# A fused attention and FFN kernel: the order of the FFN's products fixed from step 28 on instead of step 96, and a block's output evicted in two halves

## The chip, the cores and the metric

The kernel runs on one core of one Trainium2 chip. The metric is the device time of one execution in microseconds. Before the change the median of three runs is 952.14 us (951.54 to 952.98).

## The reference

The kernel computes a local and a downsampled attention over `q`, `k`, `v` (8 batches, 8 heads, 576 positions, 64 features per head), adds the two, and runs the result through a feed-forward network with a squared ReLU. All data is float32.

```
def _attn_ref(q, k, v):
    factor = 4
    q_d, k_d, v_d = ...                      # means over groups of 4 positions
    out_d = sm_attn(q_d, k_d, v_d)           # full softmax attention over 144 positions
    out_up = np.repeat(out_d, factor, axis=2)
    mask = np.abs(pos[:, None] - pos[None, :]) < factor
    scores = scale * np.matmul(q, k.transpose(0, 1, 3, 2))
    scores = np.where(mask, scores, -1000000000.0)
    ...                                      # softmax
    return out_up + np.matmul(attn, v)

def _moe_ref(x, w_in, w_out, s, b):          # x: 4608 x 512, w_in: 512 x 2048
    h = x @ w_in
    r = np.maximum(h, 0.0)
    g = s * (r * r) + b
    return g @ w_out
```

## The kernel before

**Tiling of the FFN.** The 4608 rows are cut into 18 blocks `t` of 256 rows, the 2048 hidden features into 8 parts `p` of 256. A *step* is one pair (t, p); `order` lists the 144 steps, from step 24 on simply block after block, 8 steps each, beginning with block 3. To keep float32 precision each operand is split into a high and a low float32r part, and a product is computed as three matmuls (high x high, high x low, low x high).

**One step** consists of four pieces of work, each a Python generator that a "stream" hands out in small units:

- `G`, the first products (`products1`, line 631): 24 matmuls of 256 columns into one PSUM bank `ph`. From block 3 on (with one exception in step 25) even steps use bank 4 and odd steps bank 6.
- `R` (`upper`, lines 646 to 648): ReLU, square and a rounding copy to `gh` on ScalarE. Every third step writes its pair (`gh`, `gl`) to a tile named `gb`.
- `V` (`lower`, line 653): the remainder `gl` on VectorE; after it the `ph` bank is free.
- `H`, the second products (`products2`, lines 707 to 709): 12 matmuls of 512 columns, six for the first 128 rows of the block (m = 0, PSUM bank 0 from block 3 on) and six for the other 128 rows (m = 1, bank 1). They add up over the 8 steps of a block. `H` of a step is issued one or more steps after its `G`, since `R` and `V` lie in between.

After the last `H` of a block, `evict` (line 685) computes the two halves of the output tile `os` out of the two banks with one VectorE operation each, and one DMA on SP's queue (line 687) writes the 512 KB block. The next block's products use the same two banks. The last block has an eviction of its own (line 716), in quarters.

**Attention** runs beside this. For batches 0 to 2 it is done by small matmuls (`banded`). For batches 3 to 7 the local part is done on GpSimd and VectorE (`local_unit`: GpSimd multiplies at line 537, VectorE sums at line 539, and so on), transposed by TensorE at line 569 (`ot`), and the downsampled part uses TensorE at line 342 (`sa`), lines 365 to 370 (`tp`, `tr`) and lines 381 to 383 (`up`). Before a block enters the FFN, `split_x` (lines 612 and 613) makes the high and low part of its input.

**What sets the order.** Three regimes follow one another:

1. A written plan, the string `PLAN`. Each word advances one stream; `d`, `v` and `l` with a number are pieces of attention of that unit, `G`, `R`, `V`, `H` the FFN's. `in_order` chains all instructions of TensorE, VectorE, ScalarE and GpSimd as written. The plan holds 56 `G` and 56 `H`, all of steps 0 to 27, with two units of each per step. Block 2's eviction lies in it, at the second `H` of step 23.
2. From `planned` = 28 up to `BEGIN` = 96 the loop with `until` emits the work step by step, `H` two steps behind, and the framework's planner, which simulates a timeline, decides the order on each engine by priority and simulated readiness. The first ten steps carry a dependency that puts them behind the plan (`behind_plan`).
3. From `BEGIN` on the loop runs over pairs of steps, and `products` chains TensorE's FFN matmuls in the order of emission. From here a step's `G` comes in three units (3, 9 and 12 matmuls) and its `H` in four units of 3. A pair is: 3 of `G`, 3 of `H`, 21 of `G`, 3 of `H`, 24 of `G` (the second step's), 18 of `H`. The planner still places attention's matmuls between these.

In all regimes `advance` emits attention at a rate set by the step number, and the order on each engine is fixed when the program is built.

Of the kernel before, what the change touches and what calls it, by code (L numbers as in the profile page):

```python
# [11 lines left out]
F32 = mybir.dt.float32  # L12
# [4 lines left out]
ALU = mybir.AluOpType  # L17
AX = mybir.AxisListType

P = 128  # L20
B, H, S, D = 8, 8, 576, 64
# [3 lines left out]
DM = H * D  # L25
# [11 lines left out]
TB = 256  # L37
NB = NT // TB
NFP = DFF // 256
# [47 lines left out]
def attention_ffn_kernel(ctx, tc, qk, vw_in, vr_in, vdm, qkn, vn, w_in, w_out, s_in, b_in, out):  # L87
    nc = tc.nc
# [3 lines left out]
    def pool(name, bufs, gap=0):  # L92
        if gap:
            ctx.enter_context(tc.tile_pool(name="gap_" + name, bufs=1)).tile(
                [P, gap // 4], F32, name="gap")
        return ctx.enter_context(tc.tile_pool(name=name, bufs=bufs))
# [4 lines left out]
    xp = pool("xp", 2, 0)  # L101
    xp1 = pool("xp1", 1)
# [7 lines left out]
    def bank(i, shape, name):  # L110
        return ps.tile(shape, F32, tag=f"k{i}", name=name)
# [98 lines left out]
    bias = cst.tile([P, DM], F32, name="bias")  # L210
# [408 lines left out]
    oacc = {}  # L619
# [3 lines left out]
    def products1(t, p):  # L623
# [3 lines left out]
        for j in range(2):  # L627
            f = slice(P * j, P * j + P)
            for k in range(NK):
                for s, xk in ((0, xh), (0, xl), (1, xh)):  # L630
                    nc.tensor.matmul(  # L631
                        ph[:, j], wi[p][:, s, k, f], xk[:, k],
                        start=k == 0 and s == 0 and xk is xh, stop=k == NK - 1 and s == 1)
                if j == 0 and k == 0 and order.index((t, p)) >= BEGIN:
                    yield
# [36 lines left out]
    def column_sums():  # L672
# [3 lines left out]
        nc.vector.tensor_scalar(bias, cs, sb_b, None, ALU.mult)  # L676
        yield

    def evict(t):
        if t < 2:  # L680
            os_ = xp.tile([P, 2, DM], F32, tag="xh", name="os")
        else:
            os_ = xp1.tile([P, 2, DM], F32, tag="os", name="os")
        for i in range(2):
            nc.vector.scalar_tensor_tensor(  # L685
                os_[:, i], oacc[t][i], sb_s, bias, ALU.mult, ALU.add)
        nc.sync.dma_start(
            out[TB * t : TB * t + TB, :].rearrange("(m p) c -> p m c", p=P), os_)

    def gemm2(t, p):  # L690
        for _ in products2(t, p):
            pass

    def products2(t, p):
        gh, gl = gt.pop((t, p))
        if p == 0:
            ob = OB.get(t, OB[0])
            oacc[t] = [bank(i, [P, DM], "po") for i in ob]
        po = oacc[t]
        end = t == NB - 1 and p == NFP - 1  # L700
        os_ = xp1.tile([P, 2, DM], F32, tag="os", name="os") if end else None
        for m in range(2):
            ms = slice(P * m, P * m + P)
            for j in range(2):
                first = p == 0 and j == 0
                last = p == NFP - 1 and j == 1
                nc.tensor.matmul(po[m], gh[:, j, ms], wo[p][:, 0, j], start=first, stop=False)  # L707
                nc.tensor.matmul(po[m], gh[:, j, ms], wo[p][:, 1, j], start=False, stop=False)  # L708
                nc.tensor.matmul(po[m], gl[:, j, ms], wo[p][:, 0, j], start=False, stop=last)  # L709
                if j == 0 and order.index((t, p)) >= BEGIN - 2:  # L710
                    yield
            if end:
                r0 = TB * t + P * m
                for c in (0, DM // 2):
                    cs = slice(c, c + DM // 2)
                    nc.vector.scalar_tensor_tensor(
                        os_[:, m, cs], po[m][:, cs], sb_s, bias[:, cs], ALU.mult, ALU.add)
                    nc.sync.dma_start(out[r0 : r0 + P, cs], os_[:, m, cs])
            elif p == NFP - 1 and m == 1 and t >= 2:
                evict(t)  # L720
            yield


# [11 lines left out]
    tail = {}  # L735
# [19 lines left out]
    def begin_x():  # L755
        for t in range(2):
            xs[t] = tuple(
                xp.tile([P, HP, TB], F32R, tag=tag, name=tag) for tag in ("xh", "xl"))
        for hs in (slice(0, HP - 1), slice(HP - 1, HP)):
            for t in range(2):  # L760
                xh, xl = xs[t]
                src = xt[0][:, hs, t * TB : t * TB + TB]
                nc.scalar.copy(xh[:, hs], src)
                yield
                nc.vector.tensor_tensor(xl[:, hs], src, xh[:, hs].bitcast(F32), ALU.subtract)  # L765
                yield

    def third_x():
        xs[2] = xh, xl = tuple(
            home[tag].tile([P, HP, TB], F32R, tag=tag, name=tag) for tag in ("os", "xl2"))  # L770
        for b, src, dst in ((0, slice(2 * TB, S), slice(0, S - 2 * TB)),
                            (1, slice(0, 3 * TB - S), slice(S - 2 * TB, TB))):
            nc.scalar.copy(xh[:, :, dst], xt[b][:, :, src])
            yield
            nc.vector.tensor_tensor(
                xl[:, :, dst], xt[b][:, :, src], xh[:, :, dst].bitcast(F32), ALU.subtract)
            yield

    def fourth_x():
        xs[3] = xh, xl = tuple(  # L780
            xp.tile([P, HP, TB], F32R, tag=tag, name=tag) for tag in ("xh", "xl"))
        src = xt[1][:, :, 3 * TB - S : 4 * TB - S]
        nc.scalar.copy(xh, src)
        yield
        nc.vector.tensor_tensor(xl, src, xh.bitcast(F32), ALU.subtract)
        yield

    BEGIN = 96
    order = [(t, p) for p in range(HF) for t in range(2)]
    order += [(2, 0), (2, 1)] + [(t, HF) for t in range(2)]  # L790
    order += [(2, p) for p in range(2, NFP)]
# [6 lines left out]
    sb_s = cst.tile([P, 1], F32, name="sb_s")  # L798
# [23 lines left out]
    streams = {"x": begin_x(), "y": third_x(), "z": fourth_x(), "b": add_rows()}  # L822
# [21 lines left out]
    plan = PLAN.split()  # L844
# [10 lines left out]
    @contextlib.contextmanager  # L855
    def behind_plan():

        traced = nc.cur_bb.bb.instructions
        last = traced[-1]
        yield  # L860
        start = next(k for k in reversed(range(len(traced))) if traced[k] is last) + 1
        for i in traced[start:]:
            if i.engine in ENGINES:
                tc.add_manual_dep(
                    i, tail[i.engine].name,
                    mybir.DependencyInfo(
                        mybir.DependencyClass.NoSync, mybir.DependencyReason.DATA),
                    reason="behind_plan")

    gone = {kind: plan.count(kind) for kind in "GRVH"}  # L870

    def until(kind, count):
        while gone[kind] < count:
            next(streams[kind])
            gone[kind] += 1

    chain_end = None

    def products(kind, count):

        nonlocal chain_end
        for _ in range(count):
            traced = nc.cur_bb.bb.instructions
            last = traced[-1]
            next(streams[kind])
            start = next(k for k in reversed(range(len(traced))) if traced[k] is last) + 1
            for i in traced[start:]:
                if i.engine == nc.tensor.engine:
                    if chain_end:
                        tc.add_manual_dep(  # L890
                            i, chain_end.name,
                            mybir.DependencyInfo(
                                mybir.DependencyClass.NoSync, mybir.DependencyReason.DATA),
                            reason="products")
                    chain_end = i

    def finish(st):
        with tc.high_priority():
            next(streams["R"])
            next(streams["V"])  # L900
        advance(st + 0.5)
# [32 lines left out]
    def advance(st):  # L934
        nonlocal done
        while done < target(st):
            with tc.high_priority(offset=300 if done < NY[1] else 60 if done < NY[1] + NY[2] else 0):
                if next(gen, "end") == "end":
                    break
            done += 1  # L940
# [3 lines left out]
    def split(st):  # L944
        if order[st] in splits:
            split_x(splits[order[st]])

    planned = gone["G"] // 2
    for st in range(planned, BEGIN):
        with behind_plan() if st < planned + 10 else contextlib.nullcontext():  # L950
            until("G", 2 * st + 2)
            with tc.high_priority():
                until("R", st + 1)
                until("V", st + 1)
            advance(st + 0.5)
            until("H", 2 * (st - 2))
            advance(st + 1)
            split(st)
    until("H", 2 * BEGIN - 4)
    for st in range(BEGIN, len(order), 2):  # L960
        products("G", 1)
        products("H", 1)
        products("G", 2)
        finish(st)
        products("H", 1)
        advance(st + 1)
        split(st)
        products("G", 3)
        finish(st + 1)
        products("H", 6)  # L970
        advance(st + 2)
        split(st + 1)
    products("H", 8)


# [60 lines left out]
```

## Time and profile before

| | |
|---|---|
| median of 3 runs | 952.14 us |
| profiled execution, its own time | 951.88 us |
| its span, first to last instruction | 949.8 us |
| TensorE busy | 926.5 us |
| VectorE busy | 641.0 us |
| ScalarE busy | 479.1 us |
| GpSimd busy | 410.7 us |
| mean granted TensorE clock | 0.998 |

In the profile PE is TensorE's matmuls, PEld its weight loads, DVE is VectorE, ACT ScalarE, POOL GpSimd and SP SyncE, which issues the DMAs. Times in rows are microseconds from the start of the span. A row of the chain of waits is start, length, and what the time went to; a row of instructions in order of time is start, busy time, engine, line, operation, and in brackets the idle time of the engine before it with what ended it. A row that groups instructions by line ends in count, busy microseconds, mean nanoseconds of one, and idle time before them. A row of a stage is its start and end, its length, each engine's busy time with the count of instructions, and at the end the granted clock, the share of the DMA engines that is busy, and GB/s. `ph<-xh,wi` means that `ph` is written from `xh` and `wi`. Ends of matmuls are modelled and overlap the next, so intervals between starts tell the rate.

### The profile page before, as it was taken

To read this page: it belongs to the slowest core of one execution; us is meant where nothing else is said; L and a number is where in the kernel's file an instruction comes from. 1 tells how busy PE (TensorE), PEld (TensorE's weight loads), DVE (VectorE), ACT (ScalarE), POOL (GpSimd) and SP (SyncE) were. 2 spreads that over 40 slices of the span, in tenths; PEclk is the share of its full clock that TensorE was granted. 3 is DMA by queue.
4 is the path that set the end of the run, shared out by engine and by line. 5 is a ranking of instruction groups with operands and counts; after the bars stand their busy time and mean duration, and the time that the engine had idled before them with its cause. 6 is when DMAs were issued, how large, how long until landed. Compare 5 with 4: busy or idle time off the path is not lost.

```text
span 949.8 us, 18419 instructions
## 1 busy us (share of the span) xinstructions
PE 926.5 (98%) x7316; PEld 836.1 (88%) x7316; DVE 641.0 (67%) x1134; ACT 479.1 (50%) x1133; POOL 410.7 (43%) x440
## 2 busy tenths in 40 slices
PE   6699999999999999999999999999999999999998
PEld 5588888788899999999999999999999999999996
DVE  9999999855587878787878888877887521111111
ACT  7977774466563635445454545453535333233331
POOL 6401130010577676766676877667777200000000
PEclk9999999999999999999999999999999999999999
DMA  9755413122232322323232323241312000000000
GB/s 325 268 163 191 145 46 119 50 89 91 96 118 89 118 90 86 121 80 107 80 115 92 120 87 118 67 133 51 127 62 70 1 23 1 23 1 23 1 23 22
DMA packets 31751, 86.25 MB, mean 91 GB/s; under 512 B 3249, under 2 KB 7857, under 8 KB 31665
## 3 DMA queue, kind: packets, MB, share of 16 engines
q1 hardware_dynamic: 31664, 85.08, 27.2%
q8 instruction: 57, 0.93, 0.4%
q14 instruction: 30, 0.24, 0.1%
HBM read 75.63 MB, written 9.44 MB: 90 GB/s over the span
## 4 chain that ended last, share of the span: by engine, by line
PE 85%; DVE 8%; POOL 3%; ACT 2%; issue 1%; DMA 1%; DVEq 0%; POOLq 0%; ACTq 0%
PE ph L631 38%; PE po L707 13%; PE po L708 13%; PE po L709 13%; PE sa L342 2%; PE up L383 1%; POOL pr L537 1%; PE ot L569 1%; PE ol L479 1%; DVE es L272 1%; PE up L381 1%; PE sl L436 1%; DVE es L273 1%; PE tr L370 1%; DVE gl L653 1%
## 5 line engine op out<-in xcount | busy, mean ns | idle before, releaser
L631 PE MATMUL ph<-xh,wi 128*128 128x256 f32 x2176 | 413.5, 281 | 0.1
L631 PEld LDWEIGHTS ph<-xh,wi 128*128 128x128 f32 x2176 | 344.2, 189 | 6.8 <-DVE gl L653 0.5
L631 PE MATMUL ph<-xl,wi 128*128 128x256 f32 x1152 | 322.7, 280 | 0.0
L537 POOL TENSOR_TENSOR pr<-lqk 128x576 f32<-128x576 f32 x140 | 199.0, 1444 | 76.3 <-DMA lqk<-in_qkn_dram 52.5
L631 PEld LDWEIGHTS ph<-xl,wi 128*128 128x128 f32 x1152 | 218.4, 190 | 5.9 <-DVE xl L765 0.3
L646 ACT ACTIVATE ph<-ph 128x512 f32<-128x512 f32 x144 | 83.8, 582 | 241.3 <-PE ph L631 240.8
L707 PE MATMUL po<-wo,gh 128*128 128x512 f32 x416 | 166.0, 399 | 0.7 <-DVE os L685 0.3
L708 PE MATMUL po<-wo,gh 128*128 128x512 f32 x416 | 163.8, 394 | 0.0
L709 PE MATMUL po<-wo,gl 128*128 128x512 f32 x416 | 162.6, 392 | 1.0 <-DVE gl L653 0.9
L559 POOL TENSOR_TENSOR acc<-acc,pv 128x576 f32<-128x576 f32 x80 | 117.3, 1466 | 56.7 <-DVE acc L559 30.2
L653 DVE TENSOR_TENSOR gl<-ph,gh 128x512 fp32r<-128x512 f32 x104 | 71.2, 685 | 103.9 <-ACT gh L648 103.4
L539 DVE TENSOR_REDUCE st<-pr 128x9 f32<-128x576 f32 x140 | 106.0, 757 | 38.8 <-POOL pr L537 36.3
L558 DVE TENSOR_TENSOR pv<-lv,st 128x576 f32<-128x576 f32 x120 | 86.9, 747 | 17.4 <-POOL acc L559 16.9
L312 POOL TENSOR_TENSOR dq<-vt 80x64 f32<-80x64 f32 x58 | 22.6, 401 | 174.6 <-PE up L383 173.1
L709 PEld LDWEIGHTS po<-wo,gl 128*128 128x128 f32 x416 | 78.1, 188 | 18.8 <-DVE gl L653 2.3
L707 PEld LDWEIGHTS po<-wo,gh 128*128 128x128 f32 x416 | 78.1, 188 | 14.8 <-DVE os L685 0.5
L708 PEld LDWEIGHTS po<-wo,gh 128*128 128x128 f32 x416 | 78.4, 188 | 12.2 <-issue 0.2
L647 ACT ACTIVATE ph<-ph 128x512 f32<-128x512 f32 x144 | 83.9, 582 | 3.7
L648 ACT CAST gh<-ph 128x512 fp32r<-128x512 f32 x104 | 61.0, 587 | 40.7 <-PE po L708 38.7
L653 DVE TENSOR_TENSOR gb<-ph,gb 128x512 fp32r<-128x512 f32 x40 | 27.4, 686 | 54.3 <-ACT gb L648 54.2
L708 PE MATMUL po<-wo,gb 128*128 128x512 f32 x160 | 62.8, 393 | 0.0
L707 PE MATMUL po<-wo,gb 128*128 128x512 f32 x160 | 62.7, 392 | 0.0
(158 smaller groups left out, 1240.6 us busy)
## 6 DMA issues: line engine op xcount, KB each, us to landing
tqk<-in_qk_dram SPq DMA_DIRECT2D x30, 584.0 KB, 3.8
lqk<-in_qkn_dram SPq DMA_DIRECT2D x20, 768.0 KB, 4.2
lv<-in_vn_dram SPq DMA_DIRECT2D x20, 480.0 KB, 3.4
out_dram<-os SPq DMA_DIRECT2D x17, 512.0 KB, 3.1
wst<-in_moe_w_in_dram SPq DMA_DIRECT2D x7, 1024.0 KB, 6.1
wst<-in_moe_w_out_dram SPq DMA_DIRECT2D x7, 1024.0 KB, 4.9
tvd<-in_vdm_dram SPq DMA_DIRECT2D x29, 160.0 KB, 2.4
tvr<-in_vr_dram SPq DMA_DIRECT2D x29, 128.0 KB, 2.2
```

Of the source, the lines that this page charges most:

```text
L537: nc.gpsimd.tensor_tensor(pr, lqk[:, 0:CH], lqk[:, CH + o : 2 * CH + o], ALU.mult)
L539: nc.vector.tensor_reduce(ls[:, :, o], pr, AX.X, ALU.add)
L558: nc.vector.tensor_tensor(pv, lv[:, o : o + CH], w, ALU.mult)
L559: (nc.vector if o % 3 == 1 else nc.gpsimd).tensor_tensor(acc[:, :, h], acc[:, :, h], pv, ALU.add)
L631: nc.tensor.matmul(ph[:, j], wi[p][:, s, k, f], xk[:, k], start=k == 0 and s == 0 and xk is xh, stop=k == NK - 1 and s == 1)
L646: nc.scalar.activation(ph, ph, AF.Relu)
L647: nc.scalar.activation(ph, ph, AF.Square)
L648: nc.scalar.copy(gh, ph)
L653: nc.vector.tensor_tensor(gl, acc.pop((t, p)), gh.bitcast(F32), ALU.subtract)
L707: nc.tensor.matmul(po[m], gh[:, j, ms], wo[p][:, 0, j], start=first, stop=False)
L708: nc.tensor.matmul(po[m], gh[:, j, ms], wo[p][:, 1, j], start=False, stop=False)
L709: nc.tensor.matmul(po[m], gl[:, j, ms], wo[p][:, 0, j], start=False, stop=last)
```

## The change

- `BEGIN` becomes 28, the first step behind the plan. The loop with `until` goes away; the loop over pairs takes all steps from 28 on, with the dependency on the plan for its first five pairs.
- The first pair emits no `H`, as the plan has done those of all earlier steps.
- The chain of FFN matmuls starts at the plan's last TensorE instruction.
- `evict` is cut in two: `evict_half(t, m)` evicts bank m, and writes its 128 rows with a DMA of its own (256 KB). From block 2 on it is emitted right behind the last matmul of that bank, at high priority. For blocks 0 and 1 the plan's `E` calls both halves in a row.

```
+    def evict_half(t, m):
+        if m == 0:
+            pool, tag = (xp, "xh") if t < 2 else (xp1, "os")
+            held[t] = pool.tile([P, 2, DM], F32, tag=tag, name="os")
+        os_ = held[t] if m == 0 else held.pop(t)
+        nc.vector.scalar_tensor_tensor(
+            os_[:, m], oacc[t][m], sb_s, bias, ALU.mult, ALU.add)
+        r0 = TB * t + P * m
+        nc.sync.dma_start(out[r0 : r0 + P, :], os_[:, m])
+
     def evict(t):
...
+        for m in range(2):
+            evict_half(t, m)
...
-                if j == 0 and order.index((t, p)) >= BEGIN - 2:
+                if j == 0 and order.index((t, p)) >= BEGIN:
                     yield
...
-            elif p == NFP - 1 and m == 1 and t >= 2:
-                evict(t)
+            elif p == NFP - 1 and t >= 2:
+                with tc.high_priority():
+                    evict_half(t, m)
             yield
...
-    BEGIN = 96
+    BEGIN = 28
...
-    chain_end = None
+    chain_end = tail[nc.tensor.engine]
...
-    planned = gone["G"] // 2
-    for st in range(planned, BEGIN):
-        with behind_plan() if st < planned + 10 else contextlib.nullcontext():
-            until("G", 2 * st + 2)
-            with tc.high_priority():
-                until("R", st + 1)
-                until("V", st + 1)
-            advance(st + 0.5)
-            until("H", 2 * (st - 2))
...
-    until("H", 2 * BEGIN - 4)
...
+    for st in range(BEGIN, len(order), 2):
+        begun = st > BEGIN
+        with behind_plan() if st < BEGIN + 10 else contextlib.nullcontext():
+            products("G", 1)
+            products("H", 1 * begun)
+            products("G", 2)
+            finish(st)
+            products("H", 1 * begun)
             advance(st + 1)
             split(st)
+            products("G", 3)
+            finish(st + 1)
+            products("H", 6 * begun)
+            advance(st + 2)
+            split(st + 1)
     products("H", 8)
```

More of the change, by code (lines that the diff above doesn't have):

```diff
@@ L677, in column_sums @@
         yield
-    def evict(t):
[L680 to L688, printed above, removed]
+    held = {}
+    def evict_half(t, m):
[7 more added lines that the diff above has]
+        nc.sync.dma_start(out[r0 : r0 + P, :], os_[:, m])
+    def evict(t):
+        for m in range(2):
+            evict_half(t, m)
     def gemm2(t, p):
@@ L868, in behind_plan @@
                     reason="behind_plan")
[L870 to L875, printed above, removed]
-    chain_end = None
+    chain_end = tail[nc.tensor.engine]
     def products(kind, count):
@@ L888, in products @@
                 if i.engine == nc.tensor.engine:
[L889 to L894, printed above, removed]
+                    tc.add_manual_dep(
+                        i, chain_end.name,
+                        mybir.DependencyInfo(
+                            mybir.DependencyClass.NoSync, mybir.DependencyReason.DATA),
+                        reason="products")
                     chain_end = i
@@ L946, in split @@
             split_x(splits[order[st]])
-    planned = gone["G"] // 2
-    for st in range(planned, BEGIN):
-        with behind_plan() if st < planned + 10 else contextlib.nullcontext():
-            until("G", 2 * st + 2)
-            with tc.high_priority():
-                until("R", st + 1)
-                until("V", st + 1)
-            advance(st + 0.5)
-            until("H", 2 * (st - 2))
+    for st in range(BEGIN, len(order), 2):
[6 more added lines that the diff above has]
+            products("H", 1 * begun)
             advance(st + 1)
             split(st)
-    until("H", 2 * BEGIN - 4)
[L960 to L972, printed above, removed]
+            products("G", 3)
[3 more added lines that the diff above has]
+            split(st + 1)
     products("H", 8)
```

## The prediction

> **What bounds the kernel now.** I read the page first, then the busy time by stage, then the chain of waits inside two stages. The page:
>
> ```profile
> span 949.8 us, 18419 instructions
> PE 85%; DVE 8%; POOL 3%; ACT 2%; issue 1%; DMA 1%; DVEq 0%; POOLq 0%; ACTq 0%
> ```
>
> TensorE is the bound: 85% of the chain that ended last. So the question is what changes on TensorE's own stream. I cut the span where products of steps begin (step n starts with the 24n-th first product, counted over L631): 28, 40, 88, 96, 104, 112, 120. Steps 28 to 95 are those that the change re-orders. Rows by stage, for steps 28-95, 40-87 (its undisturbed middle), 96-103, 104-111 and 112-119:
>
> ```profile
> 253.14:666.49 413.35, 412.94 (x2791) 378.99 (x2790) 330.07 (x589) 201.55 (x510) 298.36 (x277) 1.00 0.30 97
> 317.96:614.12 296.16, 296.16 (x1999) 271.93 (x1998) 234.86 (x419) 141.90 (x355) 214.71 (x202) 1.00 0.31 97
> 666.49:716.20 49.71, 49.37 (x334) 45.08 (x333) 40.25 (x75) 24.76 (x67) 36.50 (x35) 1.00 0.28 93
> 716.20:764.41 48.21, 48.21 (x328) 44.21 (x327) 30.48 (x54) 21.54 (x51) 21.64 (x19) 1.00 0.06 22
> 764.41:808.25 43.84, 43.84 (x289) 39.87 (x288) 8.16 (x11) 14.88 (x25) 0.00 (x0) 1.00 0.04 13
> ```
>
> The columns are length, busy PE, PEld, DVE, ACT, POOL, then granted clock. The clock is 1.00 everywhere, so no stage differs by throttling. PE idles for 0.4 us in 413 us: waits are not what can be saved there. What can be saved is time per product. The chain of waits in the free order, and then in the pinned order:
>
> ```profile
> 393.15 2.83 PE ph L631 x24
> ...
> 398.72 2.83 PE ph L631 x24
> ```
>
> ```profile
> 765.63 2.38 PE ph L631 x21
> ...
> 768.71 2.72 PE ph L631 x24
> ...
> 776.59 2.38 PE ph L631 x21
> ```
>
> In the free order 24 first products stand after 12 second ones (395.98 to 398.72) and take 2.83 us, 117.9 ns each. In the pinned order the run of 24 stands after only 3 second products (768.01 to 768.71) and takes 2.72 us, 113.3 ns each; the 21, also after 3, take 2.38, 113.3 too. Same shape, same clock: the rate hangs on how long the run before was. A free step lasts 398.72 - 393.15 = 5.57 us, two of them 11.14, and a pinned pair 776.59 - 765.63 = 10.96 us, so 0.18 us lie in a pair.
>
> **The change, part by part.** *1. Steps 28-95 in pinned pairs.* The stage holds 34 pairs; without attention's products the ceiling is 34 x 0.18 = 6.1 us. Attention interrupts it. Its products in the stage, grouped by line:
>
> ```profile
> L342 PE MATMUL sa<-kd,dq 128*96 128x144 f32 x102 | 16.7, 285 | 0.0
> L569 PE MATMUL ot<-ident,acc 128*128 128x128 f32 x72 | 9.2, 272 | 0.0
> L381 PE MATMUL up<-ptr,dq 128*128 128x144 f32 x32 | 6.5, 285 | 0.0
> L365 PE MATMUL tp<-ident,pd 96*80 96x96 f32 x16 | 4.0, 247 | 0.0
> ```
>
> By the code a group of `sa` has 6 products, of `ot` 9, of `up` 2 in this line, of `tp` 1: 17 + 8 + 16 + 16 = 57 groups. In every second unit `sa` and `up` stand together and interrupt once, so I count 57 - 8 = 49. A run that is cut stays slow to its end, as a pinned run shows; the first row is a group of `sa`:
>
> ```profile
> 663.40 0.73 PE sa L342 x6
> ...
> 670.79 0.46 PE ph L631 x4
> 671.50 0.25 PE tr L370 x3
> 671.75 2.38 PE ph L631 x20
> ```
>
> 0.46 + 2.38 = 2.84 for 24, no better than 2.83. I size the term by whole blocks that hold attention, since these contain interruptions. Free: 296.16 / 6 = 49.36 us per 8 steps. Pinned with attention, steps 104-111: 48.21, but one group of six `sa` fewer, 0.73 us of chain, so 48.94. Saving 0.42 per 8 steps, and 68 / 8 = 8.5 of these: **-3.6 us**. From both sides: 6.1 us if no interruption cost anything, and a loss of 3.0 if every block went like steps 96-103, 8.5 x (49.71 - 49.36). I take the later block, because the earlier one holds a stall that part 2 touches.
>
> *A page that speaks against this.* The Trainium skill, TensorE: Matmul & The Clock Gate, section Back-to-back issue gap, gives the spacing of warm matmuls by the number of columns alone: N / 2.4 + 2.5 ns, an estimate of 109 ns for 256 columns and 216 for 512, whatever stood before. By it the order of the products moves nothing and this term is 0. The trace does not agree: 113.3 and 117.9 ns stand for one shape in one run. The case is kept below as a rival.
>
> *2. The eviction in halves.* Before, bank 0's eviction is already a DVE instruction of its own, but both are queued after the last product of bank 1 was emitted. Where that hurt, at the one block boundary in steps 96-103:
>
> ```profile
> 677.99 0.40 PE L709 MATMUL po<-wo,gb 128*128 128x512 f32 x1
> ...
> 679.84 0.28 PE L631 MATMUL ph<-xh,wi 128*128 128x256 f32 x1
> 680.45 0.50 PE L707 MATMUL po<-wo,gh 128*128 128x512 f32 x1 [0.34 <-DVE os L685]
> ```
>
> ```profile
> 678.48 0.60 DVE gl L653
> 679.08 0.67 DVE st L539
> 679.75 0.66 DVE os L685
> ```
>
> Bank 0 was full at 678.39, its eviction began at 679.66 behind two DVE operations, and the next block's first product, due 0.12 us after 679.84, came at 680.45: 0.5 us of waiting, and 0.1 more in the products behind it. High priority puts the eviction ahead of `st` (0.67 us), which covers the wait: **-0.6**, from 0 if DVE is late all the same. Pinned steps 28-95 add boundaries of this kind for blocks 3 to 10, eight of them. The pinned order lets the eviction start 0.8 us late at each: bank 0 was full at 678.39 and wanted at 679.96, less 0.75 for the operation. With the eviction at the front of DVE, behind one running operation of at most 0.76, I take 0 for them, and up to 0.6 each for the range.
>
> *3. The plan's one eviction, block 2.* In the written plan the first half moves ahead of `l10 d10 l10`, in DVE's fixed order:
>
> ```profile
> 218.60 0.55 DVE L453 TENSOR_REDUCE sm<-pl 128x12 f32<-128x384 f32 x1 [0.52 <-ACT pl L451]
> ...
> 219.39 0.23 DVE L455 RECIPROCAL sm<-sm 128x12 f32<-128x12 f32 x1
> 221.18 0.75 DVE L685 SCALAR_TENSOR_TENSOR os<-po,sb_s,bias 128x512 f32<-128x512 f32 x1 [1.55 <-PE po L709]
> 222.53 0.75 DVE L685 SCALAR_TENSOR_TENSOR os<-po,sb_s,bias 128x512 f32<-128x512 f32 x1 [0.61 <-PE po L709]
> ```
>
> DVE now waits with the first half until 221.18, and L453 to L455 (218.60 to 219.62, 1.02 us) come behind it: 221.93 + 1.02 = 222.95, so the second half starts 0.42 after 222.53. From there the chain of waits runs through DVE to a TensorE transpose:
>
> ```profile
> 225.15 0.41 PE tr L370 x3
> ```
>
> So **+0.4**; 0 if DVE makes it up on the way.
>
> *4. The seam at step 28.* Pair 28/29 has no second products, and step 30's first three now stand ahead of step 28's. They need the bank that `gl` of step 28 frees:
>
> ```profile
> 259.28 0.28 PE L631 MATMUL ph<-xh,wi 128*128 128x256 f32 x1
> 259.87 0.50 PE L707 MATMUL po<-wo,gh 128*128 128x512 f32 x1 [0.32 <-ACT gh L648]
> ```
>
> ```profile
> 259.85 0.69 DVE L653 TENSOR_TENSOR gl<-ph,gh 128x512 fp32r<-128x512 f32 x1
> ```
>
> Before, TensorE waited from 259.40 to 259.87 and then had second products. Now it waits until 259.85 + 0.69 = 260.54: **+0.6**, from 0 to 1.2.
>
> *5. At nothing.* Block outputs leave in 34 transfers instead of the 17 of this row:
>
> ```profile
> out_dram<-os SPq DMA_DIRECT2D x17, 512.0 KB, 3.1
> ```
>
> A first half queued early can hold attention's loads behind it for the 1.36 us between the two evictions at 221.18 and 222.53. This delays GpSimd's sums, whose cover is tightest for block 6:
>
> ```profile
> 358.89 0.43 DVE L613 TENSOR_TENSOR xl<-x,xh 128x256 fp32r<-128x256 f32 x1
> ```
>
> ```profile
> 367.41 0.28 PE L631 MATMUL ph<-xh,wi 128*128 128x256 f32 x1
> ```
>
> Its input is split at 359.32 and used at 367.41, 8.1 us later; TensorE will come there some 1 us sooner. Without that cover a delay would show in full. Steps 112 on are pinned already and do not change.
>
> Sum: -3.6 - 0.6 + 0.4 + 0.6 = -3.2 against the profiled execution's 951.88 (span 949.8 and 2.1 around it), so 948.7; the median of the runs is 952.14, 0.26 more, so 948.9.
>
> **The rivals.** *Interruptions keep most runs slow.* If all 49 fall into different ones of the 68 long runs, 19 / 68 of 6.1 = 1.7 us are left: -1.7 - 0.6 + 0.4 + 0.6 = -1.3, 950.8. For it: the cut run above. Against: second products fill half of the time, so half of the cuts should fall there.
>
> *The order does nothing* and the rate comes from something else in the late stage: 0 for part 1, and of the stall only what part 2 saves, -0.6 + 0.4 + 0.6, 952.5. Against: steps 104-111 hold attention's products as well, with DVE busy 30.48 of 48.21 us, and are faster than the free blocks.
>
> *Slower: the boundary of blocks becomes the wait.* Every block of 8 steps has one, where the next block's first product follows three products after the last of the old. In the free order other products were put there. If DVE, 234.86 / 296.16 = 79% busy, brings bank 0's eviction more than 0.8 us late each time, each block goes like steps 96-103: +3.0 in place of -3.6 and no stall saved, +0.4 + 0.6: 956.1. It decides from about 0.4 us of stall per boundary, where 8.5 of them eat the 3.6. For it: the 0.6 at one of the two pinned boundaries under attention. Against: the priority, and that over the whole span this was the only wait of a second product for an eviction, by the view of who waited for L685:
>
> ```profile
>   PE po L707: 0.3, 1
> ```
>
> **How the numbers follow.** A measurement of this kernel can tell some 0.2%, 1.9 us, from no change. Forecast 0.60, its own range 946.6 to 950.3; interruptions 0.15; order does nothing 0.06; boundary 0.19. Faster: nearly all of the first, a third of the second, 0.62. Slower: three quarters of the boundary case, 0.15, the rest of it being half-paid stalls. Same: 0.23. The range goes down to 945.8 (6.1 us saved in part 1 whole, and the stall, with nothing lost at the seam and the plan, would be 945.4) and up to 953.5, which leaves about 0.06 below and 0.12 above.
>
> **What would show it.** Steps 28-95 in about 410 us with runs of 21 and 24 at 113.3 ns; no wait of a second product for L685's successor; the wait for `gl` at step 30 near 1.1 us; the chain through DVE at 222-225 longer by 0.4. It is wrong if runs stay at 117.9 after three second products, if the boundaries wait, or if attention's products, placed by the planner, make TensorE wait in a stage where it now never does.

## The result

The kernel after the change takes 960.07 us, the median of five runs (958.48 to 962.08), against 952.14 us (951.54 to 952.98). The ratio of the means is 1.0087, with a 95% interval of 1.0069 to 1.0104: the median is 7.9 us longer, where 3.2 us less had been forecast. The profiled execution took 959.7 us.

The page of the kernel after. The first line is the span, the second the shares of the chain that ended last, the others two groups of second products (line 712 is the old 707, line 686 the old 685):

```profile
span 957.9 us, 18429 instructions
...
PE 54%; DVE 18%; POOL 17%; issue 5%; ACT 3%; DMA 2%; DVEq 0%; POOLq 0%; ACTq 0%
...
L712 PE MATMUL po<-wo,gh 128*128 128x512 f32 x416 | 166.3, 400 | 4.6 <-DVE os L686 4.5
...
L712 PE MATMUL po<-wo,gb 128*128 128x512 f32 x160 | 63.3, 396 | 3.5 <-DVE os L686 3.5
```

TensorE's share of the chain has fallen from 85% to 54%, and GpSimd's has risen from 3% to 17%. The engine that was the bound now waits: its second products wait for the eviction, and behind that the chain runs through VectorE and GpSimd.

The busy time by stage of the kernel after, for steps 28-95, 96-103, 104-111 and 112-119, with the columns of the prediction's rows:

```profile
252.84:672.26 419.42, 412.58 (x2798) 375.74 (x2796) 338.65 (x598) 202.95 (x518) 303.42 (x280) 1.00 0.31 97
672.26:723.20 50.94, 49.52 (x336) 44.82 (x334) 39.26 (x72) 23.86 (x61) 38.48 (x36) 1.00 0.25 79
723.20:773.12 49.92, 48.02 (x325) 43.85 (x323) 27.47 (x48) 20.18 (x46) 17.21 (x16) 1.00 0.06 21
773.12:816.96 43.84, 43.84 (x290) 39.87 (x288) 8.16 (x11) 14.88 (x25) 0.00 (x0) 1.00 0.04 13
```

Steps 28-95 take 419.42 us instead of 413.35 (+6.1), and steps 96-111 take 100.86 instead of 97.92 (+2.9), although the order of their products was pinned before as well. In the first stage TensorE is idle for 6.8 us, where it was idle for 0.4. Before step 28 the kernel after is 0.3 us ahead, steps 112 to 141 take 164.40 us in both, and from the start of step 142 to the end it is 20.4 us instead of 20.9: -0.3 + 6.1 + 2.9 - 0.5 = 8.2, the difference of the spans (8.17 before rounding). The granted clock is 1.00 in every row.

What TensorE waited for from 250 to 775 us (total, times, longest):

```profile
PE po L712 <- DVE os L686: 8.0, 8, 1.9
PE ph L631 <- DVE gl L653: 1.6, 3, 1.0
PE ot L569 <- POOL acc L559: 0.2, 1, 0.2
```

These are idle times behind modelled ends. From start to start, against the usual spacing, nine boundaries of blocks cost 0.65, 0.80, 1.44, 1.23, 0.24, 0.42, 1.30, 1.30 and 2.02 us, 9.4 in all. The three waits for `gl` cost 2.1 and three for GpSimd's sums 0.9: 12.4 us, where the kernel before lost 1.2 in the same steps. The steps from 28 to 111 became 9.0 us longer with 11.2 us more of waiting, so everything else in them became some 2.2 us shorter.

One of the boundaries, at 386.78, in order of time: VectorE, then GpSimd, then TensorE. The bracket holds the idle time before the instruction and what ended it:

```profile
385.22 0.76 DVE L539 TENSOR_REDUCE st<-pr 128x9 f32<-128x576 f32 x1 [0.74 <-POOL pr L537]
385.89 0.74 DVE L686 SCALAR_TENSOR_TENSOR os<-po,sb_s,bias 128x512 f32<-128x512 f32 x1
```

```profile
383.76 2.79 POOL L537 TENSOR_TENSOR pr<-lqk 128x576 f32<-128x576 f32 x2
```

```profile
385.22 0.28 PE L631 MATMUL ph<-xh,wi 128*128 128x256 f32 x1
386.78 0.47 PE L712 MATMUL po<-wo,gh 128*128 128x512 f32 x1 [1.28 <-DVE os L686]
```

VectorE is not busy when the eviction is due. It has been idle for 0.74 us, in front of `st`, a sum of attention that needs a product from GpSimd; GpSimd delivers at 385.2. The eviction stands behind this sum in VectorE's fixed order, starts at 385.89, and TensorE goes on at 386.78. The longest wait, in the chain of waits at 738.71, has the same form:

```profile
733.85 2.78 POOL pr L537 x2
...
736.65 0.04 DVE st L539
...
737.32 0.15 DVE gl L653
...
737.92 0.75 DVE os L686
738.67 0.04 issue
738.71 0.50 PE po L712
```

The name in the wait is the eviction; what is late at these two is GpSimd. It isn't so plain at all nine. At seven VectorE had stood idle for GpSimd, by 0.28 to 1.94 us in all, just ahead of the eviction; at three of these (437.21, 636.34 and 687.56) by some 0.3 us only, where 1.23 to 1.30 us were lost. At the other two (486.48 and 535.97, 0.24 and 0.42 us) it was busy throughout. So the boundaries alone don't show the cause.

### The profile page after: what moved, and what is told of

It reads as the page before. It is cut to its first block, busy times and chain, and to the rows that moved or that the text cites. A ratio compares the mean times of both kernels' runs of the same rounds, so it can differ in the third digit from the quotient of the medians.

```text
span 957.9 us, 18429 instructions
## 1 busy us (share of the span) xinstructions
PE 924.6 (97%) x7316; PEld 831.1 (87%) x7316; DVE 645.2 (67%) x1134; ACT 478.2 (50%) x1133; POOL 412.9 (43%) x440
## 4 chain that ended last, share of the span: by engine, by line
PE 54%; DVE 18%; POOL 17%; issue 5%; ACT 3%; DMA 2%; DVEq 0%; POOLq 0%; ACTq 0%
PE ph L631 24%; PE po L712 8%; POOL pr L537 8%; PE po L713 8%; PE po L714 8%; POOL acc L559 6%; DVE pv L558 3%; DVE acc L559 2%; DVE gl L653 1%; DVE st L539 1%; DVE bias L669 1%; PE sa L342 1%; DMA lqk<-in_qkn_dram 1%; PE ol L479 1%; DVE es L272 1%
## 5 line engine op out<-in xcount | busy, mean ns | idle before, releaser
L537 POOL TENSOR_TENSOR pr<-lqk 128x576 f32<-128x576 f32 x140 | 206.4, 1495 | 77.0 <-DMA lqk<-in_qkn_dram 53.7
L559 POOL TENSOR_TENSOR acc<-acc,pv 128x576 f32<-128x576 f32 x80 | 115.0, 1437 | 54.0 <-DVE pv L558 31.5
```

Of the source, the lines that this page charges most:

```text
L537: nc.gpsimd.tensor_tensor(pr, lqk[:, 0:CH], lqk[:, CH + o : 2 * CH + o], ALU.mult)
L559: (nc.vector if o % 3 == 1 else nc.gpsimd).tensor_tensor(acc[:, :, h], acc[:, :, h], pv, ALU.add)
```

## The experiments

Two theories were set against each other from the start. **BANK**: the short distance between two blocks in the pinned order is the cause, since the next block's first product follows three products after the old block's last; give the block another bank, or more time, and the loss goes. **PACE**: GpSimd, with VectorE in a chain with it, needs some 50 us for each group of attention (one call of `local_unit`; there are ten, each ended by nine transposes `ot`), the new order of instructions puts only 8 steps of the FFN between groups, and TensorE has to wait that difference out somewhere; the boundary is merely where it stands first. Unless something else is said, an experiment is an edit of the kernel after.

### The parts alone

The pinned order with the old eviction (both halves behind the last product, one DMA, no priority):

```
-    BEGIN = 96
+    BEGIN = 28
...
             elif p == NFP - 1 and m == 1 and t >= 2:
                 evict(t)
```

> Pinned pairs from step 28, eviction as before (both halves emitted behind bank 1's last product, normal priority, one DMA). Theory BANK (in the changed kernel TensorE waits 9.4 us in all at nine boundaries because VectorE's fixed order holds the eviction behind sums that wait for GpSimd): the eviction comes no earlier than in the changed kernel, so the same waits or up to 0.7 us more at each, 960 to 966 us. Theory HALVES (the early, prioritised halves are what is wrong, the order alone is good): about 950. Theory PACE (TensorE is tied to GpSimd's pace of 50 us per group of heads): 959 to 961.

Measured: 959.84 us against 951.84, ratio 1.0084 (1.0069 to 1.0099). The waits of TensorE from 250 to 775 us:

```profile
PE po L707 <- DVE os L685: 8.6, 9, 1.9
PE ph L631 <- DVE gl L653: 1.2, 2, 1.0
```

The eviction in halves with the free order (`BEGIN = 96` and the loop with `until` kept):

```
-            elif p == NFP - 1 and m == 1 and t >= 2:
-                evict(t)
+            elif p == NFP - 1 and t >= 2:
+                with tc.high_priority():
+                    evict_half(t, m)
```

> Halves at high priority, free order up to step 96 as before. BANK and PACE: 951.5 to 952.5, since the free order puts other products between the last of a block and the first of the next; the stall of 0.6 us at 680 may go. HALVES: 954 or more, with waits for the eviction inside steps 28 to 95.

Measured: 951.47 us, ratio 0.9997 (0.9987 to 1.0007). One wait for the eviction is left, where the kernel before had one of 0.34:

```profile
PE po L712 <- DVE os L686: 0.3, 1, 0.3
```

So the whole loss belongs to the order, and the halves are worth nothing that can be measured: they neither cause the waits at the boundaries nor cover them.

### Taking the boundary away

Every second block's first half goes to bank 5 instead of bank 0, so that a new block need not wait for the old one's eviction; attention's ring of banks shrinks from three to two:

```
+OB.update((t, (5, 1)) for t in range(4, NB, 2))
...
-    ring = banks(2, 3, 5)
+    ring = banks(2, 3)
```

> The changed kernel, but every second block adds up its first 128 rows in bank 5 instead of bank 0, so the next block's first product does not need the eviction; attention has two banks in its ring instead of three. BANK: 960.1 - 9.4 = 950.7, up to 952 if attention misses its third bank. PACE: the waits move to gl and to attention's products, 955 to 959. HALVES: 950.7 too.

Measured: 959.87 us, ratio 1.0080 (1.0065 to 1.0095). No product waits for an eviction any more. The waits from 250 to 775 us (one line has been added, so line 570 is `ot`, 560 GpSimd's sum):

```profile
PE ot L570 <- POOL acc L560: 6.6, 5, 2.0
PE ot L570 <- DVE x L574: 1.3, 2, 1.0
PE ph L632 <- DVE gl L654: 1.0, 1, 1.0
```

The other way round, the bank stays, and at the first pair of a block all 24 first products go ahead of the new block's second products, which gives the eviction the time of 21 first products more:

```
+        fresh = begun and order[st - 2][1] == 0
...
+            if fresh:
+                products("G", 3)
+                finish(st)
+                products("H", 2)
```

> The changed kernel, but in the pair that opens a block 24 first products stand ahead of the next block's first second products instead of 3, so the eviction has 2.5 us more. BANK: of the nine waits (0.2 to 2.0 us each) nothing is left, each such pair loses 0.1 us by a slow run: 960.1 - 9.4 + 0.9 = 951.6. PACE: 955 to 959, waits on gl instead.

Measured: 961.26 us, ratio 1.0096 (1.0081 to 1.0111). Here too the evictions are no longer waited for. The first three of attention's groups that wait (`ot`, the first transposes that need GpSimd's finished sums), in order of time:

```profile
303.43 1.21 PE L569 MATMUL ot<-ident,acc 128*128 128x128 f32 x9 [0.17 <-POOL acc L559]
354.19 1.20 PE L569 MATMUL ot<-ident,acc 128*128 128x128 f32 x9 [1.36 <-POOL acc L559]
404.50 1.20 PE L569 MATMUL ot<-ident,acc 128*128 128x128 f32 x9 [0.90 <-POOL acc L559]
```

and from 250 to 775 us together:

```profile
PE ot L569 <- POOL acc L559: 8.9, 7, 2.5
```

BANK falls in both. Two quite different ways of freeing the boundary leave the time within 1.2 us of the kernel after, and most of the wait moves to the next instruction of TensorE that hangs on GpSimd. PACE expected the move, but a time of 955 to 959 us: the loss stayed whole. The 1.3 us at `x` in the first of the two, the sum that empties attention's banks, may come from the smaller ring.

### Changing the pace

These three leave part of the work out. In the first two GpSimd forms the local scores over only half of the 64 features, and VectorE's sum takes only that half; once on the kernel after and once on the kernel before. In the third only VectorE's sum is halved and GpSimd does all its work.

```
                 nc.gpsimd.tensor_tensor(
-                    pr, lqk[:, 0:CH], lqk[:, CH + o : 2 * CH + o], ALU.mult)
-                nc.vector.tensor_reduce(ls[:, :, o], pr, AX.X, ALU.add)
+                    pr[:, :, 0 : D // 2], lqk[:, 0:CH, 0 : D // 2],
+                    lqk[:, CH + o : 2 * CH + o, 0 : D // 2], ALU.mult)
+                nc.vector.tensor_reduce(ls[:, :, o], pr[:, :, 0 : D // 2], AX.X, ALU.add)
```

> The changed kernel with half of GpSimd's score products left out (each L537 product and the sum L539 behind it takes 32 of 64 features, so the scores are not the reference's). Theory PACE (the order of instructions allows TensorE 8.0 steps per group of heads, GpSimd delivers a group every 50.3 us, and 8 pinned steps with attention need 48.9, so TensorE waits 1.4 us per group, wherever the order puts the first thing that needs GpSimd): a group now takes GpSimd some 40 us, TensorE never waits for it, and the pinned order shows its gain: 947 to 950, and 2 to 4 us less than the kernel before with the same half left out. Theory ORDER (the pinned order is itself worse for TensorE when attention runs): 955 or more, and 4 or more above the kernel before with the half left out.

> The kernel before with the same half of GpSimd's score products left out. PACE: TensorE waited for nothing in steps 28 to 95 before either, so 950.5 to 952.5. ORDER: the same.

> The changed kernel with VectorE's sums alone made lighter (L539 sums 32 of the 64 features, so the scores are not the reference's); GpSimd does all its work. The planner now puts 7.6 to 8.0 steps between the groups. PACE: GpSimd is as slow as before, so the waits stay or grow: 959 to 966. Theory BACKLOG (VectorE itself, 79% busy, is what comes late): 0.33 us less on each of 140 sums, the waits shrink by half or more: 955 or less.

Measured, with the kernel before at 952.24 on that chip: the lightened kernel after 953.68 (ratio 1.0014, 1.0005 to 1.0023); the lightened kernel before 951.78 (0.9997, 0.9987 to 1.0006); the kernel after with only the sums lightened 968.69 (1.0172, 1.0154 to 1.0190).

The first missed what PACE had expected, 947 to 950. The penalty of the pinned order shrinks from 7.9 to 1.9 us, but it doesn't turn into a gain. With shorter operations the planner also changed the order: over the first seven groups it put one on every 7.0 steps instead of 8.0, and they came 44.1 us apart. TensorE's waits from 250 to 775 us are 4.5 us in this run, and none of them stands at `ot`, so it isn't shown that GpSimd's pace is behind what is left. The test is confounded and only its direction counts.

In the third a group stands on every 7.7 steps in the order of instructions (7.65 of `G`, 7.72 of `H`), and GpSimd's pace hardly followed: its last sums of the first and the last group end 48.8 us per group apart, while 7.7 steps of the FFN with attention need 7.7 x 6.14 = 47.3 us (6.14 from 49.1 us per 8 steps, measured below). The time, 16.5 us above the kernel before, lies even above the 959 to 966 us that PACE had expected. The waits at the eviction alone:

```profile
PE po L712 <- DVE os L686: 13.5, 8, 3.1
```

Leaving out work of VectorE, on whose queue the late eviction stands, made the kernel 8.6 us slower than the kernel after. That speaks against a backlog on VectorE, the third theory in the expectations, but it doesn't rule it out, for the order changed too. Ahead of four of the eight evictions that were waited for, VectorE had itself waited 1.2 to 2.0 us for GpSimd within the last 3 us; ahead of the other four it was at work on its part of the softmax and the weighted values. From the third group on TensorE came to the groups 2.3 to 4.3 us after GpSimd's last sum. How much of this loss is GpSimd's pace and how much the new order on VectorE, the run doesn't tell.

### Moving attention later

The order stays pinned and no work is left out, but from the third group on the instructions of attention on TensorE and VectorE are put, by dependencies that only fix the order, behind the step where a group falls at 8.35 steps per group:

```
+    RATE, FIRST, BASE = 8.35, 2, 45.67
...
+        mark = marks[min(max(marks), int(BASE + RATE * (k - FIRST)) - 1)]
...
+            if i.engine in mark:
+                tc.add_manual_dep(
+                    i, mark[i.engine].name,
```

> The changed kernel with attention of batches 4 to 7 kept back: its VectorE and TensorE instructions are put behind the FFN's of a step that advances 8.35 steps per group, so that in the order of instructions the groups stand 8.3 to 8.4 steps apart instead of 8.0. Nothing else is changed and no work is left out. PACE: 8.35 steps take TensorE about 51 us, more than GpSimd's 50.3, so the waits of batches 4 to 7 go: 960.1 - 9.4 = 950.7, between 949 and 953. ORDER and BACKLOG: 958 to 962.

Measured: 951.06 us, ratio 0.9993 (0.9983 to 1.0002). The loss of 7.9 us is gone, by moving attention alone. VectorE has as much to do as before, so a backlog, which had expected 958 to 962, falls here as well. The waits from 250 to 775 us, then the busy time of three blocks of 8 steps (48-55, 56-63 and 104-111):

```profile
PE ph L631 <- DVE gl L653: 1.0, 1, 1.0
PE po L712 <- DVE os L686: 0.7, 1, 0.7
PE ot L569 <- POOL acc L559: 0.5, 1, 0.5
```

```profile
371.93:421.07 49.14, 49.14 (x334) 45.20 (x333) 38.24 (x70) 22.18 (x57) 33.71 (x32) 1.00 0.31 100
421.07:470.09 49.02, 49.02 (x334) 44.96 (x333) 39.73 (x72) 24.24 (x63) 36.54 (x34) 1.00 0.32 100
...
714.32:763.35 49.03, 49.03 (x334) 44.97 (x333) 38.34 (x71) 23.59 (x61) 29.61 (x24) 1.00 0.15 50
```

What is left of the waits stands before step 48: the seam at 260.67, and 286.77, 336.05 and 354.15, 2.9 us in all. From step 48 on TensorE is busy in all of 49.14, 49.02 and 49.03 us, and the whole gain of the pinned order can be seen. The same delay on the kernel before shows whether moving attention is itself worth something:

```
+    RATE, FIRST, BASE = 8.35, 2, 46.17
```

> The kernel before (free order up to step 96, eviction as before) with attention of batches 4 to 7 kept back at 8.35 steps per group. PACE: the free order needs 50.0 us for its 8.1 steps per group and GpSimd as much, so TensorE waited for nothing and there is nothing to win: 951.5 to 953. If keeping attention back is worth something by itself, apart from undoing the waits of the pinned order: 950 or less.

Measured: 952.07 us against 951.82, ratio 1.0002 (0.9993 to 1.0010). It is worth nothing by itself; it cures a loss that only the pinned order has.

### Trying for a version that beats both

Pinned only from step 48 on, to leave out the stretch in which waits remained, with and without attention kept back:

```
-    BEGIN = 28
+    BEGIN = 48
```

> Free order up to step 48 as in the kernel before, pinned pairs from 48, eviction in halves, and attention of batches 4 to 7 kept back at 8.35 steps per group. In the run with attention kept back from step 28 on, steps 48 to 111 took 391.4 us against 397.0 before, of which 2.75 are second products done earlier, and TensorE's waits that were left (2.9 us) all lay before step 48. Theory PACE: without these, 952.1 - 2.8 = 949.3, between 948.5 and 950.5. If the shorter products are worth nothing once attention is kept back: 951.5 to 952.5.

> The same with attention not kept back: the order of instructions has 8.0 steps per group again from group 3 on. PACE: the pinned steps need 48.9 us and GpSimd 50.3 per group, eight groups from step 46 on, so up to 8 x 1.4 = 11 us of waits on top of the 949.3: 956 to 960. If pinning from 48 instead of 28 is what helps: 949 to 951.

Measured, with the kernel before at 951.87: kept back 952.55 (1.0004, 0.9995 to 1.0012), not kept back 955.69 (1.0038, 1.0026 to 1.0049). The second, just below the 956 to 960 expected, has waits like those of the kernel after again, but fewer:

```profile
PE po L712 <- DVE os L686: 3.4, 4, 1.6
```

The first was expected at 948.5 to 950.5 and missed. The 3.1 us between the two have the sign that PACE expected, at less than half of its size; but small waits are left in the first, and their form is new. In this kernel's waits `st` at lines 545 and 547 belongs to the softmax of a group:

```profile
PE po L712 <- DVE st L547: 1.6, 3, 0.6
...
PE po L712 <- DVE st L545: 0.3, 1, 0.3
```

The third to seventh groups fall at steps 56.6, 64.6, 72.8, 80.8 and 88.5, just behind the boundaries at 56, 64, 72, 80 and 88, so that their softmax stands next to the evictions on VectorE. That reading comes from the trace and was not tried.

Last, pinned from 28 with attention kept back, and the early waits attacked at their places: 24 first products ahead of the second ones at steps 34 and 42, second products first at step 30:

```
+        fresh = begun and st < 46 and order[st - 2][1] == 0
...
+                if st == BEGIN + 2:
+                    products("H", 1)
+                    products("G", 1)
```

> The changed kernel with attention of batches 4 to 7 kept back at 8.35 steps per group, as in the run that came to 951.06 us, and its left-over waits before step 48 attacked: in the pairs at steps 34 and 42 24 first products stand ahead of the next block's second ones, and at step 30 second products go first. Of the 1.2 us at step 30 some 0.6 remain; the 0.25 and 0.9 at the two block boundaries go. 951.1 - 1.7 = 949.4, between 948.5 and 950.5, below the kernel before. If waits only move on to the next thing that GpSimd feeds before step 48: 950.5 to 951.5.

Measured: 952.08 us against 951.82, ratio 1.0002 (0.9993 to 1.0011); the 949.4 expected was missed, and so were the 950.5 to 951.5 for waits that move on. The seam fell from 1.19 to 0.46 us and the boundaries at steps 32 and 40 no longer wait, but at the second group of attention there is a wait of 1.8 us instead of 0.5:

```profile
354.12 1.20 PE L569 MATMUL ot<-ident,acc 128*128 128x128 f32 x9 [1.79 <-POOL acc L559]
```

GpSimd delivers the second group at 354.1 us, as it did without these edits (354.1). What TensorE saves before that, it waits there. No version measured is faster than the kernel before by more than the noise.

## Why the prediction was wrong

**The step that failed** is the line in part 2 on the eight new boundaries, "I take 0 for them": seven of them waited, 6.1 us in all, and the two at steps 96 and 104, pinned before as well, 3.3, together 9.4 us. Behind it stands a wrong view of what an eviction waits for. I set the slack of 0.8 us against one running operation of VectorE, at most 0.76 us, and took priority to mean the front of the queue. The queue's order is fixed when the program is built, by the planner's simulated times; on the chip an operation ahead of the eviction can itself be waiting, and at 385.22 it was.

**The cause one step further back** is part 5, where GpSimd went in at nothing. I looked at when each block's input is needed (8.1 us of cover for block 6), not at the rate at which groups come. The groups `ot`, grouped over the whole kernel, before and then after (90 products, nine to a group; first and last start):

```profile
L569 PE MATMUL ot<-ident,acc x90: 270/273/273, 304.5 to 755.0; 128*128 128x128 f32 x90
```

```profile
L569 PE MATMUL ot<-ident,acc x90: 270/273/331, 303.3 to 756.9; 128*128 128x128 f32 x90
```

With the last group's start at 754.1 and 756.0, TensorE comes to a group every 50.0 us before and every 50.3 after. Who sets this pace shows in the distance from GpSimd's last sum of a group (line 559) to the group's first transpose. At the second group, before and then after:

```profile
347.74 2.96 POOL L559 TENSOR_TENSOR acc<-acc,pv 128x576 f32<-128x576 f32 x2 [1.53 <-DVE pv L558]
355.10 1.14 PE L569 MATMUL ot<-ident,acc 128*128 128x128 f32 x9
```

```profile
350.66 2.95 POOL L559 TENSOR_TENSOR acc<-acc,pv 128x576 f32<-128x576 f32 x2 [1.53 <-DVE pv L558]
353.67 1.20 PE L569 MATMUL ot<-ident,acc 128*128 128x128 f32 x9 [0.20 <-POOL acc L559]
```

Before, the sums end at 350.70 and TensorE comes 4.4 us later; after, they end at 353.61 and it starts 0.06 us later. Over the ten groups the distance was 1.0 to 4.4 us before; in the kernel after it is 0.05 to 1.0 us in the first nine. So GpSimd was a little ahead before, and after the change TensorE reaches the groups just as GpSimd delivers. GpSimd's last sums come 49.8 us per group apart before and 50.1 after, so its own pace did not rise. It is set by dependencies between GpSimd and VectorE, by loads, and in a small part by TensorE: in the kernel after GpSimd waits 14.2 us for TensorE's `up` between 303 and 757 us (11.7 before). VectorE's waits for GpSimd from 253 to 735 us, before and after:

```profile
DVE st L539 <- POOL pr L537: 36.3, 44, 1.7
DVE pv L558 <- POOL acc L559: 15.4, 14, 3.3
```

```profile
DVE st L539 <- POOL pr L537: 44.0, 50, 2.2
DVE pv L558 <- POOL acc L559: 31.2, 21, 3.1
```

In the kernel before, 8.1 steps stand between two groups in the order of the instructions (counted in the trace, 8.04 of `G` and 8.17 of `H`), and at 49.34 us per 8 steps TensorE needs 50.0 us for them, about the pace of GpSimd, so TensorE doesn't wait. In the kernel after, 8.0 steps stand there, and at 49.1 us per 8 steps TensorE would need 49.1. Of these 0.9 us some 0.6 come from the groups standing closer in the order, and some 0.2 from faster products. Against the measured 50.3 TensorE is ahead by 1.2 us per group, 10.8 in nine; 12.4 us of waits were measured, 1.9 of them before the first group, which leaves 10.5. (The two figures are no independent check, for the 50.3 are intervals of TensorE itself and hold its waits.) At 7.7 steps per group the loss was larger; at 8.35, where TensorE needs 51.3 us, it was gone. GpSimd's part of the chain, 3%, and its 43% of busy time had told me that it has room. The 43% are of the whole span; in steps 28-95 it was 298.36 of 413.35 us, 72%, and its chain has waits of its own, so there was no room for a TensorE that needs its groups sooner.

**Term 1 was mis-sized, with the sign right.** In the kernel with attention kept back, steps 48 to the end take 573.0 us against 577.6 before. Of these 4.6 us (from the start of step 48 to the last product), 2.8 are 12 second products that the pinned order does earlier, and 0.3 are less waiting at the boundaries; the remaining 1.5 us were saved in the six re-ordered blocks, 0.25 us per 8 steps and not 0.42. The kernel after shows much the same: some 2.2 us saved beside the waits, in 68 re-ordered steps. For the 8.5 blocks that is -2.1 instead of -3.6. I had taken the price from the one late block, which at 48.94 us was better than the blocks above at 49.02 to 49.14. The rates themselves are as predicted. In the chain of waits of the kernel with attention kept back:

```profile
507.77 2.38 PE ph L631 x21
510.15 0.23 PE po L712
510.38 0.98 PE ot L569 x9
511.37 0.23 PE po L713
511.60 0.23 PE po L714
511.83 2.71 PE ph L631 x23
```

The run of 21 takes 113.3 ns each, and the run of 23, after an interruption among the three second products ahead of it, 117.8. Between 372 and 764 us, 608 of the 1392 first products in runs of ten or more went at the faster rate before (by the median interval of their run), 1044 of 1320 in this kernel, and 1253 of 1325 in the kernel after. So the order does what it was thought to do, but 44% of the free order's products were fast already, which I had not counted, and a cut in the short run of three can spoil the long run behind it, as here. By its size the rival of the interruptions (1.7 us) was nearer.

The Trainium skill, TensorE: Matmul & The Clock Gate, section Back-to-back issue gap, gives N / 2.4 + 2.5 ns, a formula by the number of columns alone, as the gap of an isolated matmul, and says that in a stream of weight loads and matmuls both set the spacing. The prediction left this second half out. The two rates for one shape above disagree with the formula in all three of these kernels; whether the weight loads make the difference, no run here shows.

**The small terms.** The seam at step 28 was right: the forecast wait was near 1.1 us, and the trace has 1.04 us of idle time, 1.20 from start to start, for `gl`:

```profile
260.30 0.38 PE L631 MATMUL ph<-xh,wi 128*128 128x256 f32 x1 [1.04 <-DVE gl L653]
```

The plan's block 2 went as described, in part: the first half now stands ahead of lines 453 to 455 on VectorE, and the second half starts 1.59 us behind the first instead of 1.35. That is 0.24 us and not the 0.4 forecast. Steps 24-27, in which the chain goes on through VectorE to TensorE, took 30.22 us against 30.06, so 0.16 us of it reached TensorE; the halves alone have 30.23, the order alone 30.06. The -0.6 for the stall at the boundary in steps 96-103 was wrong: with the halves alone 0.3 of 0.34 us is left. In that run's trace `st` (679.28) still stands ahead of the eviction (679.94) on VectorE, so the priority did not put the eviction first.

**The rivals.** The slower one named the right place and sign, at half of the size: with its own +3.0 for the stage, +0.4 and +0.6 it came to 956.1, 4.0 us of the 7.9. But its mechanism, a VectorE too busy to bring the eviction in time, was not the cause of most of the loss: the two kernels without the boundary's wait are as slow, and keeping attention back takes no work from VectorE and removes the loss. "The order does nothing" falls with the counts of the rates above. The last sentence of the prediction, that attention's products placed by the planner could make TensorE wait, was the true one, and it stood without a price or a chance.

**What stays open.** Why the planner puts 8.0 steps between groups in the pinned order and 8.1 in the free one was not seen, since its simulated times are in no trace. GpSimd's own pace was only changed together with the planner's placing, and it is no constant: with the order pinned from step 48 and attention not kept back the groups came every 49.5 us. In the kernel after, 40.0 us of GpSimd's idle time between 303 and 757 us are waits for one load of attention (`lqk`, a single buffer), as many as before; whether a second buffer would lift the pace was not tried.

## What to carry to other kernels

Before an engine that is busy all the time is made faster or its work is put in a new order, work out for each engine that feeds it how long a unit of its work takes, waits included, and compare that with the time that the bound engine will need for the work standing between two such units in the fixed order; a feeder that is far from busy all the time can be in step already, so take its busy share from the stage and not from the whole span, and look at how long its results lie ready before they are used. When a wait disappears on one line and the time stays, look for it at the next instruction that depends on the same feeder. The name in a wait is the last link, so read what the named engine was itself waiting for just before.

## What the runs showed of the hardware

The rate of a run of first products depends on what stands before it: some 113 ns each behind a few second products, 118 behind many. Of the first products in long runs between 372 and 764 us, all 501 that stood behind eight or more second products were slow in the kernel before, and 1030 of 1062 behind three that followed other first products were fast in the kernel after; behind an interruption by attention both rates occur. The granted clock was 1.00 in these stretches, and why it is so, no run here shows. Also unexpected was that less work on one engine can cost time: halving VectorE's sums, with nothing else changed in the source, made the kernel 8.6 us slower (968.69 against 960.07). The planner placed the groups closer, 7.7 steps apart instead of 8.0, and GpSimd's last sums still came 48.8 us apart; that this alone is the reason was not shown.
